# Decay products shifted by one token: transfers of 112 and 15 rows, a second matmul for three chunks, and loads issued at the end of a turn

## The chip, the cores and the metric

The kernel runs on one NeuronCore of a Trainium2 chip. The core has TensorE (PE, with its weight loads PEld), VectorE (DVE), ScalarE (ACT), GpSimd (POOL) and SyncE (SP), and 16 DMA engines that all of them share. The metric is the time of one execution on the device, in microseconds, as the median of several runs. The profile and the trace come from one profiled execution.

## The reference

The first half is a linear attention with a decay (RWKV-6), for 4 batches, 8 heads, 768 tokens and a head size of 48. For every token the state of a head, 48x48, is scaled row by row by `w` and gets `k v` added:

```python
for t in range(S):
    cur = einsum('bhd,bhe->bhde', u[None] * kt, vt)
    y[:, :, t] = einsum('bhd,bhde->bhe', rt, state + cur)
    state = wt[:, :, :, None] * state + einsum('bhd,bhe->bhde', kt, vt)
```

The second half (mixture of depths) takes `y` as `x`, 768 tokens of 384 numbers in each batch. It scores each token by `x @ w_gate`, picks the 128 best of a batch, sends them through `relu(xe @ w1) @ w2` (384 to 1024 to 384), and adds the result, times a sigmoid of the score, to these tokens.

## The kernel before

The 768 tokens of a batch are cut into 6 chunks of 128 tokens (L = 128), so there are N = 24 chunks. A chunk has its tokens on the 128 partitions and 8 heads x 48 in the free dimension: 384 numbers of 4 bytes, 1,536 bytes a row.

The product of decays inside a chunk is made with logarithms. `lnw` takes ln of `w` on ScalarE (L134). `sums` multiplies it on TensorE with the triangular matrix `tri` (L143), which gives for each token the sum of logarithms from that token to the chunk's end. ScalarE takes exp of it as `fall` (L146) and exp of its negative as `rise` (L152). The rows of `fall` then go to two places by DMA:

- L150, issued by ScalarE: rows 1 to 127 of `fall` go to rows 0 to 126 of `e_buf`, since key `t` needs the product of the decays after it. Row 127 of the three `e_buf` tiles is set to 1 once, at the start.
- L151, issued by SyncE: row 0, the decay over the whole chunk, goes to the DRAM tile `lines`. `whole` (L162) reads it back, turned, into `all_buf`, with two transfers for each chunk but a batch's first.

`scaled` (L193) makes K = k x e_buf and R = r x rise on VectorE. `turned` (L204) transposes both on TensorE, ScalarE copies them out (L206). `scores` (L224), `fresh` (L240), `masked` (L252), `states` (L265 to L272, the last one on GpSimd with `all_buf`), `from_state` (L283) and `from_chunk` (L301) make the chunk's output in PSUM. `result` (L323 to L333) writes it out and computes the token scores. `own_products`, `own_sum` and `own_values` do the term with `u`, mostly on GpSimd.

The order is written by hand (`manual_schedule`): every engine runs its instructions in program order. A loop of turns `n` from -4 to 23 does step `turned` for chunk n+2, `scores` to `states` for n+1, `from_state`, `from_chunk` and `result` for n, `scaled` for n+3 and `sums` for n+4, `lnw` for n+5. From turn 6 on, the steps of the second half for the batch before (`mixture`, 28 steps) are spread over the turns, 4 or 5 in each; those of the last batch follow the loop.

SyncE issues in a turn: the four loads of chunk n+8 (L105; `w`, `k`, `r`, `v`, 192 KB each in pieces of 192 bytes), in turns 0 to 6 a slab of the second half's weights (L526), the two `whole` transfers of chunk n+3, the store of chunk n's output (L333), and the row of chunk n+4 (L151). ScalarE issues L150. The head of the program loads chunks 0 to 3 (18 transfers, with `u` and `w_gate`) before the first turn. The tiles for loads have 5 buffers for `w`, 7 for `k` and `r`, 10 for `v`; `fall` and `rise` have 2, `e_buf` 3.

Of the kernel before, what the change touches and what calls it, by code (L numbers as in the profile page):

```python
# [9 lines left out]
FP32 = mybir.dt.float32  # L10
# [3 lines left out]
AF = mybir.ActivationFunctionType  # L14
ALU = mybir.AluOpType
AX = mybir.AxisListType

L = 128
HB = 64
LIMIT = 1e15  # L20


def _rows(ap, n):

    return dataclasses.replace(ap, ap=[[0, n]] + [list(x) for x in ap.ap])
# [10 lines left out]
def kernel(  # L36
# [14 lines left out]
    nc = tc.nc  # L51
# [3 lines left out]
    C = H * D  # L55
# [13 lines left out]
    consts = ctx.enter_context(tc.tile_pool(name="consts", bufs=1))  # L69
# [5 lines left out]
    psR = ctx.enter_context(tc.tile_pool(name="psR", bufs=3, space=PSUM))  # L75
# [3 lines left out]
    N = len(chunks)  # L79
    views = dram_disjoint_views(out, B)  # L80

    lines = dram.tile([N, C], FP32, name="lines")
# [12 lines left out]
    work = {n: {} for n in range(N)}  # L95

    def load(n, names="wkrv"):
        if n >= N:
            return
        b, ci = chunks[n]  # L100
        for name in names:
            x, bufs = dict(w=(w, 5), k=(k, 7), r=(r, 7), v=(v, 10))[name]
            t = lev.tile([L, H, D], FP32, tag=name, name=name, bufs=bufs)
            src = x[b, :, ci * L:(ci + 1) * L, :].rearrange("h t d -> t h d")
            nc.sync.dma_start(out=t, in_=src)  # L105
            work[n][name] = t
# [7 lines left out]

    ident = consts.tile([L, L], FP32)
    tri = consts.tile([L, L], FP32)
    mask = consts.tile([L, HB], FP32)
    ones = consts.tile([L, 1], BF16)
    ones_f = consts.tile([L, 1], FP32)
# [4 lines left out]
    row = setup.tile([L, L], INT32)  # L124
    col = setup.tile([L, L], INT32)
# [4 lines left out]
    def lnw(n):  # L130
        if n < N:
            t = work[n]
            t["lw"] = lev.tile([L, C], FP32, tag="lw", name="lw", bufs=2)
            nc.scalar.activation(  # L134
                out=t["lw"], in_=t.pop("w").rearrange("p h d -> p (h d)"), func=AF.Ln
            )

    def sums(n):
        if not 0 <= n < N:
            return  # L140
        t = work[n]
        ps = psR.tile([L, 512], FP32, tag="r", name="ps_x")
        nc.tensor.matmul(ps[:, 0:C], tri, t.pop("lw"), start=True, stop=True)  # L143
        fall = t["fall"] = lev.tile([L, C], FP32, tag="fall", name="fall")
        rise = t["rise"] = lev.tile([L, C], FP32, tag="rise", name="rise")
        nc.scalar.activation(  # L146
            out=fall, in_=ps[:, 0:C], func=AF.Exp, accum_out=guard[:, n, 0:1]
        )
        e = t["e"] = e_bufs[n % len(e_bufs)]
        nc.scalar.dma_start(out=e[0:L - 1], in_=fall[1:L])  # L150
        nc.sync.dma_start(out=lines[n:n + 1], in_=fall[0:1])  # L151
        nc.scalar.activation(  # L152
            out=rise, in_=ps[:, 0:C], func=AF.Exp, scale=-1.0, accum_out=guard[:, n, 1:2]
        )

    def whole(n):
        if not 0 <= n < N or chunks[n][1] == 0:
            return
        t = work[n]["all"] = all_bufs[n % len(all_bufs)]
        line = lines[n].rearrange("(j q d) -> q d j", q=2, d=D)  # L160
        for par in (0, 1):
            nc.sync.dma_start(out=t[HB * par:HB * par + D, :], in_=line[par])  # L162
# [16 lines left out]
    def own_values(n):  # L179
        if not 0 <= n < N:  # L180
            return
        t = work[n]
        t["vo"] = lev.tile([L, H, D], FP32, tag="vo", name="vo")
        nc.gpsimd.tensor_mul(t["vo"], t["v"], t.pop("own").to_broadcast([L, H, D]))  # L184

    def scaled(n):
        if not 0 <= n < N:
            return
        t = work[n]
        t["K"] = k_bufs[n % len(k_bufs)]  # L190
        t["R"] = r_bufs[n % len(r_bufs)]
        for to, of, by in (("K", "k", "e"), ("R", "r", "rise")):
            nc.vector.tensor_mul(  # L193
                t[to][:, :, 0:D], t.pop(of), t.pop(by).rearrange("p (h d) -> p h d", d=D)
            )
# [18 lines left out]
    def half(i, n=HB):  # L214
        return slice(HB * i, HB * i + n)
# [58 lines left out]
    def from_state(n):  # L274
        if not 0 <= n < N:
            return
        t = work[n]
        begun = set()
        for j in range(HP):
            for par, sub in quarters:  # L280
                if sub == 0 and chunks[n][1] == 0:
                    continue
                nc.tensor.matmul(  # L283
                    t["P"][half(sub), par, j * D:(j + 1) * D],
                    t["Rt"][half(par, D), j, half(sub)],
                    t["s1" if sub else "s0"][half(par, D), j, :],
                    start=(par, sub) not in begun, stop=False, skip_group_check=True,
                )
                begun.add((par, sub))
# [176 lines left out]
    def run(*steps):  # L466
        for g in steps:
            yield from g
# [5 lines left out]
            next(mixing, None)  # L474

    per_turn = [5, 5, 5, 4, 5, 4]
    AHEAD = 8

    with tc.manual_schedule():
        nc.scalar.preload_act_table_set("natural_log_exp_and_others")  # L480
        load(0, "wkr")
        load(1, "wkr")
        nc.sync.dma_start(out=u_bc, in_=_rows(u, L))
        load(0, "v")
        load(1, "v")
        load(2)
        nc.sync.dma_start(out=wg_bc, in_=_rows(moe_w_gate, L))
        load(3)

        nc.gpsimd.iota(row, pattern=[[1, L]], base=0, channel_multiplier=0)  # L490
        nc.gpsimd.iota(col, pattern=[[0, L]], base=0, channel_multiplier=1)
        nc.vector.tensor_tensor(out=tri, in0=col, in1=row, op=ALU.is_ge)
        for t in e_bufs:
            nc.gpsimd.memset(t[L - 32:L], 1.0)
        nc.vector.tensor_tensor(out=ident, in0=col, in1=row, op=ALU.is_equal)
        for t in k_bufs + r_bufs:
            nc.vector.memset(t[:, :, D:HB], 0.0)
        for t in all_bufs:
            nc.gpsimd.memset(t, 1.0)
        nc.vector.tensor_tensor(out=behind[:, 0:L], in0=col, in1=row, op=ALU.is_lt)  # L500
        for i in (0, 1):
            nc.vector.tensor_copy(out=mask[half(i)], in_=behind[half(i), half(i)])
            nc.vector.memset(p_bufs[i], 0.0)
        nc.vector.tensor_copy(out=slots, in_=row)
        nc.vector.memset(ones, 1.0)
        nc.vector.memset(ones_f, 1.0)
        nc.gpsimd.memset(behind[:, L:S], 1.0)
        nc.gpsimd.iota(count, pattern=[[-L, NCH]], base=S - 1, channel_multiplier=-1)
        nc.vector.tensor_copy(out=behind_n, in_=count)
        nc.gpsimd.iota(  # L510
            number[:, :, :, 0], pattern=[[S, B], [L, NCH]], base=0, channel_multiplier=0
        )
        nc.gpsimd.iota(
            number[:, :, :, 1], pattern=[[0, B], [0, NCH]], base=0, channel_multiplier=1
        )
        nc.vector.tensor_copy(out=ids, in_=number)

        lnw(0)
        for n in range(-4, N):
            if n >= 0 and chunks[n][1] == 0 and n > 0:  # L520
                mixing = run(mixing, mixture(chunks[n][0] - 1))
            k1 = per_turn[chunks[n][1]] if n >= NCH else 0
            load(n + AHEAD)
            if n >= 0 and n < len(weights):
                to, of = weights[n]
                nc.sync.dma_start(out=to, in_=of)  # L526
            whole(n + 3)
            lnw(n + 5)
            from_state(n)
            turned(n + 2)  # L530
            scores(n + 1)
            fresh(n + 1)
            own_values(n + 1)
            masked(n + 1)
            states(n + 1)
            mix(k1 // 2)
            from_chunk(n)
            result(n) if n >= 0 else None
            own_products(n + 3)
            own_sum(n + 2)  # L540
            sums(n + 4)
            scaled(n + 3)
            mix(k1 - k1 // 2)
        mixing = run(mixing, mixture(B - 1))
        mix(1000)

        total = setup.tile([L, 1], FP32)
        nc.vector.tensor_reduce(out=total, in_=guard, axis=AX.XY, op=ALU.add)
        ps = psM.tile([L, C], FP32, tag="m", name="ps_w")
        nc.tensor.matmul(ps[0:1, 0:1], total, ones_f, start=True, stop=True)  # L550
        wide = setup.tile([1, 1], INT32)
        nc.vector.tensor_scalar(
            out=wide, in0=ps[0:1, 0:1], scalar1=LIMIT, scalar2=0.5, op0=ALU.is_le, op1=ALU.is_lt
        )
# [72 lines left out]
```

## Time and profile before

| | us |
|---|---|
| median of 3 runs | 379.18 (373.69 to 379.99) |
| the profiled execution | 376.85 |
| its span | 374.8 |
| PE busy | 215.0 (57%) |
| DVE busy | 137.0 (37%) |
| POOL busy | 94.3 (25%) |
| ACT busy | 76.8 (20%) |
| granted TensorE clock, mean | 0.751 of full speed |

The profiled execution took 376.85 us, and 374.8 us of them lie in the span that the trace shows. No engine is busy for much more than half of it. The span falls into a head (until the first chunks are through), 20 turns in which chunks 3 to 23 get their K (from 64.05 us to 317.73 us), and a tail of 57.1 us with the last outputs and the second half of the last batch.

### The profile page before, as it was taken

How to read it: one execution, taken by the hardware profiler on the slowest of the kernel's cores; microseconds unless marked ns; L12 is line 12 of the kernel's file. 1: busy time of each engine (PE TensorE's matmuls, PEld its weight loads, DVE VectorE, ACT ScalarE, POOL GpSimd, SP SyncE). 2: the span in 40 equal slices, each digit the busy share in tenths (PEclk: the TensorE clock that was granted, in tenths of full speed). 3: DMA queues.
4: the chain of work that ended last, by engine and by line, in shares of the span. 5: the costliest groups of instructions: out<-in, count | busy, mean ns of one | idle time of the engine just before them, and what ended most of it. 6: DMA issues, size and time to landing. Idle time of an engine off the chain costs nothing.

```text
span 374.8 us, 8418 instructions
## 1 busy us (share of the span) xinstructions
PE 215.0 (57%) x3586; PEld 168.3 (45%) x3586; DVE 137.0 (37%) x329; ACT 76.8 (20%) x195; POOL 94.3 (25%) x119
## 2 busy tenths in 40 slices
PE   3033252645536745057997337579698647994581
PEld 1023141535425534045865326468465547862460
DVE  4011114404404442615334137353246666326100
ACT  3011411302202321112232221222223211101010
POOL 4300003304307030344330340543215344101101
PEclk9995556875855786565999685669779867997596
DMA  7555716156266515828036542554212111001000
GB/s 149 118 119 118 156 45 130 39 144 163 63 153 160 140 34 112 196 55 194 24 85 137 119 106 63 141 129 91 64 37 64 47 46 51 24 23 42 23 0 30
DMA packets 117100, 34.07 MB, mean 91 GB/s; under 512 B 108864, under 2 KB 116288, under 8 KB 117056
## 3 DMA queue, kind: packets, MB, share of 16 engines
q1 hardware_dynamic: 113472, 27.21, 33.7%
q10 hardware_dynamic: 3072, 4.68, 3.5%
q0 software_dynamic: 512, 1.57, 1.3%
q8 instruction: 30, 0.49, 0.6%
q14 instruction: 14, 0.11, 0.1%
HBM read 23.23 MB, written 5.54 MB: 77 GB/s over the span
## 4 chain that ended last, share of the span: by engine, by line
DMA 47%; PE 24%; issue 5%; SPq 5%; DVE 3%; ACT 2%; POOL 2%; ACTq 0%; POOLq 0%; DVEq 0%
DMA e_buf<-fall 29%; DMA lines<-fall 7%; PE ps_h L440 6%; DMA xe<-out_dram,idx 5%; PE ps_p L301 5%; DMA all_buf<-lines 4%; PE ps_f L450 3%; PE ps_t L204 3%; PE ps_x L143 3%; SPq L162 2%; PE ps_p L224 2%; SPq L105 1%; DVE k_buf L193 1%; PE ps_p L240 1%; DMA w<-in_moe_w_dram 1%
## 5 line engine op out<-in xcount | busy, mean ns | idle before, releaser
L204 PE MATMUL ps_t<-ident,k_buf 128*128 128x128 f32 x96 | 21.6, 366 | 68.4 <-DVE k_buf L193 68.4
L272 POOL TENSOR_TENSOR s<-mid,all_buf 128x192 f32<-128x192 f32 x20 | 10.5, 524 | 186.8 <-DMA all_buf<-lines 127.8
L204 PEld LDWEIGHTS ps_t<-ident,k_buf 128*128 128x128 f32 x96 | 13.9, 182 | 72.9 <-issue 40.5
L252 DVE TENSOR_TENSOR sc<-ps_p,mask 128x512 f32<-128x512 f32 x24 | 16.6, 691 | 65.0 <-PE ps_p L240 64.9
L193 DVE TENSOR_TENSOR k_buf<-k,e_buf 128x384 f32<-128x384 f32 x24 | 14.6, 609 | 64.6 <-DMA e_buf<-fall 64.6
L301 PE MATMUL ps_p<-v,sc 64*64 64x48 f32 x768 | 34.8, 253 | 0.0
L301 PEld LDWEIGHTS ps_p<-v,sc 64*64 64x64 f32 x768 | 32.1, 169 | 5.5 <-issue 4.6
L143 PE MATMUL ps_x<-lw,tri 128*128 128x384 f32 x48 | 28.3, 680 | 8.7 <-ACT lw L134 5.6
L440 PE MATMUL ps_h<-xeT,w 128*128 128x128 f32 x192 | 31.2, 323 | 3.4 <-ACT hid L445 2.8
L283 PE MATMUL ps_p<-s,Rt 48*64 48x48 f32 x704 | 19.3, 247 | 22.5 <-DVE mid L270 15.1
L440 PEld LDWEIGHTS ps_h<-xeT,w 128*128 128x128 f32 x192 | 28.9, 232 | 6.8 <-ACT hid L445 3.6
L146 ACT ACTIVATE fall<-ps_x 128x384 f32<-128x384 f32 x24 | 11.8, 490 | 94.8 <-PE ps_x L143 39.3
L184 POOL TENSOR_TENSOR vo<-v,own 128x384 f32<-128x384 f32 x24 | 22.8, 950 | 33.2 <-DVE own L177 33.1
L283 PEld LDWEIGHTS ps_p<-s,Rt 48*64 48x64 f32 x704 | 16.2, 158 | 32.9 <-POOL s L272 17.6
L450 PE MATMUL ps_f<-w,hid 128*128 128x384 f32 x64 | 25.6, 533 | 2.7 <-ACT hid L445 2.1
L206 ACT COPY Kt<-ps_t 128x512 f32<-128x512 f32 x24 | 14.0, 584 | 64.1 <-PE ps_t L204 64.0
L169 POOL TENSOR_TENSOR rk<-r,k 128x384 f32<-128x384 f32 x24 | 26.0, 1084 | 2.5 <-DMA r<-in_r_dram 2.5
L170 POOL TENSOR_TENSOR rk<-rk,u_bc 128x384 f32<-128x384 f32 x24 | 25.0, 1040 | 5.4 <-DMA u_bc<-in_u_dram 3.6
L323 DVE TENSOR_TENSOR x<-ps_p,vo 128x384 f32<-128x384 f32 x24 | 13.3, 554 | 26.9 <-PE ps_p L301 24.2
L224 PE MATMUL ps_p<-Rt,Kt 48*64 48x64 f32 x768 | 22.8, 279 | 0.0
L224 PEld LDWEIGHTS ps_p<-Rt,Kt 48*64 48x64 f32 x768 | 18.8, 183 | 6.0 <-issue 6.0
L204 PE MATMUL ps_t<-ident,r_buf 128*128 128x128 f32 x96 | 21.1, 361 | 0.2 <-DVE r_buf L193 0.2
(75 smaller groups left out, 271.0 us busy)
## 6 DMA issues: line engine op xcount, KB each, us to landing
w<-in_w_dram SPq DMA_DIRECT2D x24, 192.0 KB
k<-in_k_dram SPq DMA_DIRECT2D x24, 192.0 KB
r<-in_r_dram SPq DMA_DIRECT2D x24, 192.0 KB
v<-in_v_dram SPq DMA_DIRECT2D x24, 192.0 KB
out_dram<-x SPq DMA_DIRECT2D x24, 192.0 KB
e_buf<-fall ACTq DMA_DIRECT2D x24, 190.5 KB
w<-in_moe_w_dram SPq DMA_DIRECT2D x3, 512.0 KB
w<-in_moe_w_dram SPq DMA_DIRECT2D x4, 384.0 KB
```

What stands on the lines that cost most here:

```text
L143: nc.tensor.matmul(ps[:, 0:C], tri, t.pop("lw"), start=True, stop=True)
L169: nc.gpsimd.tensor_mul(rk, t["r"], t["k"])
L170: nc.gpsimd.tensor_mul(rk, rk, u_bc)
L184: nc.gpsimd.tensor_mul(t["vo"], t["v"], t.pop("own").to_broadcast([L, H, D]))
L193: nc.vector.tensor_mul(t[to][:, :, 0:D], t.pop(of), t.pop(by).rearrange("p (h d) -> p h d", d=D))
L204: nc.tensor.transpose(ps[:, j, :], t[name][:, 2 * j:2 * j + 2, :], ident)
L224: nc.tensor.matmul(P[half(sub), par, j * HB:(j + 1) * HB], t["Kt"][half(par, D), j, half(sub)], t["Rt"][half(par, D), j, half(sub)], start ...
L252: nc.vector.tensor_mul(t["sc"], t["P"][:, :, 0:SC].rearrange("p q (j t) -> p q j t", t=HB), _heads(mask, 2, HP),)
L283: nc.tensor.matmul(t["P"][half(sub), par, j * D:(j + 1) * D], t["Rt"][half(par, D), j, half(sub)], t["s1" if sub else "s0"][half(par, D), ...
L301: ins = nc.tensor.matmul(t["P"][half(sub), par, j * D:(j + 1) * D], t["sc"][half(sub), par, j, :], t["v"][half(sub), 2 * j + par, :], star ...
L440: nc.tensor.matmul(ps[:, q, :], w1[:, dc, (f0 + q) * L:(f0 + q + 1) * L], xeT[:, dc, :], start=(dc == 0), stop=(dc == NDC - 1),)
L450: nc.tensor.matmul(ps, hid[:, fc, :], w2[:, fc, :], start=(fc == 0), stop=(fc == NFC - 1))
```

## The change

```diff
--- before.py
+++ after.py
@@ -18,6 +18,7 @@
 L = 128
 HB = 64
 LIMIT = 1e15
+EARLY = 3
 
 
 def _rows(ap, n):
@@ -114,6 +115,7 @@
 
     ident = consts.tile([L, L], FP32)
     tri = consts.tile([L, L], FP32)
+    tri_s = consts.tile([L, L], FP32)
     mask = consts.tile([L, HB], FP32)
     ones = consts.tile([L, 1], BF16)
     ones_f = consts.tile([L, 1], FP32)
@@ -140,18 +142,27 @@
             return
         t = work[n]
         ps = psR.tile([L, 512], FP32, tag="r", name="ps_x")
-        nc.tensor.matmul(ps[:, 0:C], tri, t.pop("lw"), start=True, stop=True)
+        nc.tensor.matmul(ps[:, 0:C], tri, t["lw"], start=True, stop=True)
         fall = t["fall"] = lev.tile([L, C], FP32, tag="fall", name="fall")
         rise = t["rise"] = lev.tile([L, C], FP32, tag="rise", name="rise")
         nc.scalar.activation(
             out=fall, in_=ps[:, 0:C], func=AF.Exp, accum_out=guard[:, n, 0:1]
         )
         e = t["e"] = e_bufs[n % len(e_bufs)]
-        nc.scalar.dma_start(out=e[0:L - 1], in_=fall[1:L])
-        nc.sync.dma_start(out=lines[n:n + 1], in_=fall[0:1])
+        if n < EARLY:
+            strict = psR.tile([L, 512], FP32, tag="r", name="ps_x")
+            nc.tensor.matmul(strict[:, 0:C], tri_s, t["lw"], start=True, stop=True)
+            nc.scalar.activation(out=e, in_=strict[:, 0:C], func=AF.Exp)
+        else:
+            for lo, hi in ((0, L - 16), (L - 16, L - 1)):
+                nc.scalar.dma_start(out=e[lo:hi], in_=fall[lo + 1:hi + 1])
         nc.scalar.activation(
             out=rise, in_=ps[:, 0:C], func=AF.Exp, scale=-1.0, accum_out=guard[:, n, 1:2]
         )
+
+    def line(n):
+        if 0 <= n < N:
+            nc.sync.dma_start(out=lines[n:n + 1], in_=work[n]["fall"][0:1])
 
     def whole(n):
         if not 0 <= n < N or chunks[n][1] == 0:
@@ -474,7 +485,7 @@
             next(mixing, None)
 
     per_turn = [5, 5, 5, 4, 5, 4]
-    AHEAD = 8
+    AHEAD = 7
 
     with tc.manual_schedule():
         nc.scalar.preload_act_table_set("natural_log_exp_and_others")
@@ -492,6 +503,7 @@
         nc.vector.tensor_tensor(out=tri, in0=col, in1=row, op=ALU.is_ge)
         for t in e_bufs:
             nc.gpsimd.memset(t[L - 32:L], 1.0)
+        nc.vector.tensor_tensor(out=tri_s, in0=col, in1=row, op=ALU.is_gt)
         nc.vector.tensor_tensor(out=ident, in0=col, in1=row, op=ALU.is_equal)
         for t in k_bufs + r_bufs:
             nc.vector.memset(t[:, :, D:HB], 0.0)
@@ -520,7 +532,6 @@
             if n >= 0 and chunks[n][1] == 0 and n > 0:
                 mixing = run(mixing, mixture(chunks[n][0] - 1))
             k1 = per_turn[chunks[n][1]] if n >= NCH else 0
-            load(n + AHEAD)
             if n >= 0 and n < len(weights):
                 to, of = weights[n]
                 nc.sync.dma_start(out=to, in_=of)
@@ -539,6 +550,8 @@
             own_products(n + 3)
             own_sum(n + 2)
             sums(n + 4)
+            line(n + 4)
+            load(n + AHEAD)
             scaled(n + 3)
             mix(k1 - k1 // 2)
         mixing = run(mixing, mixture(B - 1))
```

Four things change in it.

1. For chunks 3 to 23 the transfer of 127 rows becomes two, of rows 1 to 112 and 113 to 127, both issued by ScalarE, in place of the one.
2. For chunks 0 to 2 there is no transfer. A second matmul with `tri_s` (strictly greater) gives the sums that leave the token itself out, and ScalarE takes their exp straight into `e_buf`. `tri_s` is one more comparison on VectorE at the start.
3. The row that goes to `lines` is issued by a call of its own, `line(n + 4)`, right behind `sums(n + 4)`: it stays behind the output's store on SyncE's queue.
4. The loads move from the start of a turn to its end, behind `line`, and are of chunk n+7 in place of n+8. In turn -4 that is chunk 3, which the head of the program loads too (L488, not in the diff).

## Rows read from the trace of the kernel before

**Rows 1.** The page: the chain that ended last, shares of the span by line
```profile
DMA e_buf<-fall 29%; DMA lines<-fall 7%; PE ps_h L440 6%; DMA xe<-out_dram,idx 5%; PE ps_p L301 5%; DMA all_buf<-lines 4%; PE ps_f L450 3%; PE ps_t L204 3%; PE ps_x L143 3%; SPq L162 2%; PE ps_p L224 2%; SPq L105 1%; DVE k_buf L193 1%; PE ps_p L240 1%; DMA w<-in_moe_w_dram 1%
```

**Rows 2.** Waits, all engines: engine, line <- releaser: us in total, times, longest
```profile
DVE k_buf L193 <- DMA e_buf<-fall: 64.6, 15, 14.1
```

**Rows 3.** Waits of SyncE's queue, same columns
```profile
SPq L105 <- DMA e_buf<-fall: 45.6, 5, 9.7
```

**Rows 4.** DMA view: queues (packets, MB, share of 16 engines) and issues
```profile
q1 hardware_dynamic: 113472, 27.21, 33.7%
q10 hardware_dynamic: 3072, 4.68, 3.5%
...
e_buf<-fall ACTq DMA_DIRECT2D x24, 190.5 KB
```

**Rows 5.** Chain in order of time: start us, us, what
```profile
178.82 0.61 PE ps_p L283 x32
...
220.85 14.31 DMA e_buf<-fall
...
275.30 10.44 DMA e_buf<-fall
...
337.69 1.85 DMA out_dram<-x
```

**Rows 6.** Windows: per engine busy us (instructions), granted clock, DMA share, GB/s
```profile
0.00:20.00 20.00, 3.29 (x4) 1.00 (x4) 4.49 (x19) 4.37 (x10) 6.84 (x23) 1.00 0.63 127
...
80.00:120.00 40.00, 17.88 (x324) 14.31 (x328) 12.97 (x25) 8.23 (x21) 13.89 (x15) 0.61 0.59 145
...
280.00:300.00 20.00, 15.00 (x326) 11.29 (x317) 12.90 (x27) 5.89 (x16) 7.62 (x9) 0.93 0.17 54
```

**Rows 7.** Timeline, chunk 13's transfer: start, us, engine, line, operation, [idle before]
```profile
186.48 0.61 ACTq L150 DMA_DIRECT2D e_buf<-fall  x1
...
187.10 0.68 PE L283 MATMUL ps_p<-s,Rt 48*64 48x48 f32 x32
...
195.76 2.68 SPq L333 DMA_DIRECT2D out_dram<-x  x1
...
198.44 0.56 DVE L193 TENSOR_TENSOR k_buf<-k,e_buf 128x384 f32<-128x384 f32 x1 [3.18 <-DMA e_buf<-fall]
...
204.59 0.49 ACT L146 ACTIVATE fall<-ps_x 128x384 f32<-128x384 f32 x1 [2.52 <-PE ps_x L143]
```

**Rows 8.** Timeline: k_buf products of chunks 3, 4, 5, 6 and 19 to 23
```profile
64.05 0.70 DVE L193 TENSOR_TENSOR k_buf<-k,e_buf 128x384 f32<-128x384 f32 x1
...
73.35 0.56 DVE L193 TENSOR_TENSOR k_buf<-k,e_buf 128x384 f32<-128x384 f32 x1 [1.86 <-DMA e_buf<-fall]
...
88.43 0.70 DVE L193 TENSOR_TENSOR k_buf<-k,e_buf 128x384 f32<-128x384 f32 x1
...
98.84 0.56 DVE L193 TENSOR_TENSOR k_buf<-k,e_buf 128x384 f32<-128x384 f32 x1 [1.98 <-DMA e_buf<-fall]
...
274.67 0.55 DVE L193 TENSOR_TENSOR k_buf<-k,e_buf 128x384 f32<-128x384 f32 x1
...
285.76 0.56 DVE L193 TENSOR_TENSOR k_buf<-k,e_buf 128x384 f32<-128x384 f32 x1 [0.44 <-DMA e_buf<-fall]
...
295.71 0.56 DVE L193 TENSOR_TENSOR k_buf<-k,e_buf 128x384 f32<-128x384 f32 x1 [2.14 <-DMA e_buf<-fall]
...
304.33 0.56 DVE L193 TENSOR_TENSOR k_buf<-k,e_buf 128x384 f32<-128x384 f32 x1 [0.85 <-DMA e_buf<-fall]
...
317.73 0.55 DVE L193 TENSOR_TENSOR k_buf<-k,e_buf 128x384 f32<-128x384 f32 x1
```

**Rows 9.** Groups by form: prefix-sum matmuls, busy us, mean ns, idle before
```profile
L143 PE MATMUL ps_x<-lw,tri 128*128 128x384 f32 x48 | 28.3, 680 | 8.7 <-ACT lw L134 5.6 <-ACT rise L152 3.1
```

**Rows 10.** Timeline, head: chunk 2's w load and its ln
```profile
7.71 2.89 SPq L105 DMA_DIRECT2D w<-in_w_dram  x1
...
18.90 0.52 ACT L134 ACTIVATE lw<-w 128x384 f32<-128x384 f32 x1 [9.31 <-DMA w<-in_w_dram]
```

## Prediction, made before the changed kernel was run

> **What bounds the kernel now.** I read the chain of work that ended last first. No engine leads it: the transfer `e_buf<-fall` holds 29% of the span, some 109 us, and the one-row transfer to `lines` 7% [rows 1]. The reader is to see that this is a latency, since the waits say the same from the other side: VectorE stood 64.6 us before its k_buf product, 15 times, for this transfer alone [rows 2]. SyncE's queue, which loads the next chunks, is also put down as waiting for it, 45.6 us [rows 3].
>
> Why is it slow? The queue table answers [rows 4]. ScalarE's queue, q10, did 3,072 packets for 24 transfers: 128 each, that is 127 rows and one more. On q1, I counted the pieces of data: 98,304 for 96 loads, 3,072 for stores, 7,680 for `all_buf` (40 transfers of 192 numbers), 384 + 1,024 for the weights, 256 for the two broadcasts and 24 for `lines`, in all 110,744. What is left of 113,472 is 2,728, and that is exactly 16 for each of 169 transfers and 1 for each of 24 one-row transfers. So a transfer leaves one closing packet on each DMA engine that it uses. A load uses 16, a single row one, and the 127 rows one as well. A q10 packet took 3.5% x 16 x 374.8 / 3,072 = 68 ns, so 128 of them take 8.75 us on one engine. With some 1.7 us around them that is the 10.44 us of the quietest case; beside loads it is up to 14.31 [rows 5].
>
> That one DMA engine is full. In the first 20 us loads moved 127 x 20 = 2,540 KB, less 195 of chunk 0's shifted rows: 147 KB on each engine, 763 pieces of 192 B. A q1 packet took 33.7% x 16 x 374.8 / 113,472 = 17.8 ns, so that is 13.6 us; with 8.75 it is 22 us of work in 20 for the one engine, and about 14 for the others, whose mean share was 0.63 [rows 6]. So loads end late there too.
>
> The timeline of chunk 13 shows the way it goes around: issued at 186.48, landed at 198.44 (12.0), k_buf, and 6.2 us later the next-but-one `fall` at 204.59, which needs that turn's transposes and matmuls before it on TensorE. The store at 195.76 is held 2.68 us, to the moment when chunk 13's rows land, though it doesn't read them [rows 7]. In program order it is the eighth transfer of SyncE and ScalarE behind them. I read this as eight completion counters used in turn.
>
> **The change, part by part.**
>
> *Two transfers for one.* 112 rows divide evenly over 16 engines, as the loads' 128 do, 15 don't. The nearest row for a transfer that uses 16 is the store of 128 rows of the same 1,536 bytes: 1.85 us [rows 5]; that is the lower bound. The upper one is no change, 12. The 15 rows, on one engine, cost 15 x 68 ns = 1.0 on top of 1.7, and their issue waits 0.61 for the first one's [rows 7]. Sum: 0.6 + 2.7, about 3.5 us with some contention. I take that, because beside loads the old transfer gained at most 14.31 - 10.44 = 3.9 us over 128 packets, 30 ns each, and the new one has 8 on an engine. ScalarE gains one issue, 0.61 us in a turn, under its 20% busy time.
>
> The Trainium skill, "DMA: Bandwidth & Descriptors", section "Why a DMA increments its semaphore by 16 and not by 1", says that a transfer uses the largest number of engines up to 16 that divides its slowest dimension, so 16 for 112 and 15 for 15; its 127 to 1 agrees with the closing packets [rows 4]. By it the second part costs 0.9 us less, and the sum would be the same, since neither price sets the turn. Speaking against the change, "Queues, rings and completion order" there says that an engine goes around its queues by packets of about 9 to 17 descriptors; seven packets would then wait 1.1 to 2.1 us (9 to 17 times 17.8 ns, an estimate), which is small too.
>
> The loop around it falls from 12.0 + 6.7 (with the exp's 0.5) to 3.5 + 6.7 = 10.2 us for two turns, 5.1 a turn. Turns took (317.73 - 64.05) / 20 = 12.7 [rows 8], so something else is late next: TensorE's own turn.
>
> *A turn without that wait.* I take the waits out of measured turns. Without the second half: chunks 3 to 4, 9.30 - 1.86 = 7.4, and 5 to 6, 10.41 - 1.98 = 8.4 [rows 8]; mean 7.9. Weight slabs load there (7 slabs, 3.1 MB, at full rate up to 2.2 us a turn); I add 0.9 of these 0 to 2.2. Six turns: 6 x 8.8 = 53 (48 to 61). With the second half, a batch of six: 9.95 - 2.14 = 7.8, 8.62 - 0.85 = 7.8 and 13.4 (the gather stall, which stays) [rows 8], twice 8.28 (from state product to state product, 178.82 to 187.10) [rows 5, 7], and 11.09 - 0.44 = 10.7 [rows 8]: 56.2. I take 57 (54 to 60) with loads beside it, two times. The last two turns, 22.0 - 0.85 = 21. The tail stays at 374.8 - 317.73 = 57.
>
> *Head.* Three transfers of 127 rows go, so the full DMA engine goes. Added are three pairs of matmuls, 0.68 each [rows 9], three exps at 0.49 and one comparison: some 2 us for each chunk, under the wait for `w` (9.31 before chunk 2's ln [rows 10]); uncovered it is 6 us. Chunk 3 is loaded twice, 786 KB. Before turn 0's copies ScalarE takes ln of chunk 5, behind 18 + 4 + 4 + 1 = 27 transfers of 196.6 KB, 5.31 MB. The rate at full share is 127 / 0.63 = 202 GB/s [rows 6]: 26 us at share 1, 42 at 0.63. I take 0.85, 31 us, and 5 for the start and turn 0: chunk 3's k_buf at 36 (29 to 44), against 64.05.
>
> *Loads two chunks later.* SyncE's order stays (row, loads, weights, `whole`, store), only the chunk is two lower, and `w` comes one turn and a bit before its ln. The worst `w` took from 7.71 to 18.90 = 11.2 us [rows 10], with the full engine; a turn covers 8 of it, and without cover it would cost 3 a turn. Nothing in the sum. With ten transfers in a turn the eighth-before rule makes the 15 rows wait for `w` of the turn before, with `rise`, ln and the copies queued behind it on ScalarE; it was issued a turn earlier, so nothing either.
>
> Sum: 36 + 53 + 57 + 57 + 21 + 57 = 281 us of span, against 374.8. With 2.05 around it (376.85 - 374.8) the profiled time would be 283; the median stands 2.3 above the profiled one, so 286.
>
> **Rivals.**
>
> *The DMA engines become the bound.* Both queues did 37.2% x 374.8 = 139 us of work for 16 engines; the second load of chunk 3 adds 4. At the head's share of 0.63 to 0.65 [rows 6] this takes 220 us up to chunk 23's loads, which chunk 21's turn needs at 203 in my sum: 225 + 21 + 57 + 4 = 308; at 0.59 [rows 6] 330. For it: loads come in a burst behind each turn's end. Against: the share was low because one engine was full.
>
> *It doesn't spread.* If the parts still run on one engine or a few, only the head's 28 us are gained: 351. Against: the loads' closing packets.
>
> *Quicker.* TensorE had a granted clock of 0.61 from 80 to 120 us, with waits in it, and 0.93 from 280 to 300 [rows 6]. With the clock at 2.4 GHz nearly throughout, turns fall to 7: 29 + 42 + 50 + 50 + 20 + 55 + 4 = 250.
>
> *Slower: `w` comes too late.* From the loads' issue to ln is one turn, and behind ln ScalarE has the copies, `fall` and so the next row and loads: two turns take the latency of `w` plus 7. To be slower than now by 2% (387) turns must take (387 - 4 - 36 - 57) / 20 = 14.5, a latency of 22 us. At 24 it would be 407. The longest measured is 11.2 [rows 10].
>
> **How the numbers follow.** Chances: forecast (272 to 302) 0.62; DMA bound (300 to 330) 0.19; quicker (250 to 272) 0.09; no spread (340 to 360) 0.07; slower 0.03. The predicted time is 286; the range 264 to 322 takes in most of the second and half of the third. About 2% is what a measurement here can tell from no change. All but the last are faster by more: 0.94; within 2% 0.03, for a `w` late by nearly that much; slower 0.03.
>
> **What would show it.** ScalarE's queue should show closing packets of 16 for the 112 rows, and the time from its issue to k_buf some 3.5 us; the e_buf wait should leave the top of the chain, with PE lines in its place. Chunk 3's k_buf should stand near 36 us, turns near 8.8 and 9.5. Wrong would be: waits of k_buf on `e_buf` as long as before, ln waiting for `w` in every turn, or a DMA share near 0.65 throughout with TensorE waiting.

## The result and the profile after

The changed kernel takes 280.81 us, the median of 4 runs (279.03 to 286.5); the kernel before took 376.55 in the runs beside it. The ratio is 0.746, with a 95% interval of 0.734 to 0.758. The forecast was 286 (264 to 322). The profiled execution has a span of 277.2 us, where the sum gave 281.

The page of the changed kernel, first the engines' busy time and then the chain that ended last, by line (L204 is now the k_buf product, L215 the transposes, L106 the loads, L136 ln):

```profile
PE 201.8 (73%) x3592; PEld 153.6 (55%) x3592; DVE 141.2 (51%) x330; ACT 76.9 (28%) x198; POOL 96.8 (35%) x119
...
PE ps_t L215 6%; SPq L106 6%; PE ps_h L451 6%; DMA w<-in_w_dram 5%; PE ps_p L312 5%; PE ps_p L235 4%; PE ps_f L461 4%; DVE r_buf L204 4%; DVE ahead L369 3%; PE ps_x L145 3%; DVE k_buf L204 3%; PE ps_p L251 3%; DVE x L334 2%; DMA e_buf<-fall 2%; DVE sc L263 2%
```

The transfer of shifted rows, 29% of the chain before [rows 1], stands at 2%. In its place several lines of TensorE, VectorE and SyncE's queue stand close together, none above 6%. The DMA view of the same kernel (queue: packets, MB, share of 16 engines' span):

```profile
q1 hardware_dynamic: 117632, 28.00, 47.0%
q10 hardware_dynamic: 3318, 4.10, 5.1%
```

3,318 packets on ScalarE's queue are 158 for each of 21 chunks: 127 rows and 31 closing packets. With at most 16 a transfer, that is 16 for the 112 rows and 15 for the 15 rows. A packet takes 5.1% x 16 x 277.2 / 3,318 = 68 ns, as before [rows 4], so nothing got faster; the rows run side by side. On q1 there are 4,160 packets more than before: 4 x (1,024 + 16), the second load of chunk 3.

Two transfers from the chain in order of time (start us, us, what), and a load for comparison:

```profile
45.36 2.37 DMA e_buf<-fall
...
61.38 3.84 DMA e_buf<-fall
...
68.31 6.25 DMA w<-in_w_dram
```

The two pairs that stand in the chain are through after 2.4 and 3.8 us, against 10.4 to 14.3 for the one transfer [rows 5]. The waits (engine, line <- releaser: us in total, times, longest):

```profile
ACT lw L136 <- DMA w<-in_w_dram: 23.0, 8, 7.2
POOL s L283 <- DMA all_buf<-lines: 22.8, 4, 9.1
...
PE ps_t L215 <- DVE k_buf L204: 9.3, 12, 1.5
```

The wait of the k_buf product for the transfer, 64.6 us before [rows 2], is gone from the list; TensorE waits 9.3 us for k_buf in all. What is at the top of the waits for transfers now is `w`: ln stood 23.0 us for it. GpSimd's wait for `all_buf`, the way of the one-row transfer, was the longest of all before and has shrunk as well, from 127.8 us to 22.8. The line of the kernel before:

```profile
POOL s L272 <- DMA all_buf<-lines: 127.8, 9, 37.9
```

The timeline gives the time of the k_buf product of chunks 3, 9, 15, 21 and 23:

```profile
36.34 0.88 DVE L204 TENSOR_TENSOR k_buf<-k,e_buf 128x384 f32<-128x384 f32 x1
...
86.89 0.55 DVE L204 TENSOR_TENSOR k_buf<-k,e_buf 128x384 f32<-128x384 f32 x1
...
141.92 0.54 DVE L204 TENSOR_TENSOR k_buf<-k,e_buf 128x384 f32<-128x384 f32 x1
...
196.61 0.54 DVE L204 TENSOR_TENSOR k_buf<-k,e_buf 128x384 f32<-128x384 f32 x1
...
217.96 0.54 DVE L204 TENSOR_TENSOR k_buf<-k,e_buf 128x384 f32<-128x384 f32 x1
```

And the windows (busy us and instructions of PE, PEld, DVE, ACT and POOL, then granted clock, DMA share, GB/s):

```profile
0.00:36.00 36.00, 18.64 (x248) 11.74 (x248) 13.73 (x38) 12.93 (x34) 12.41 (x30) 0.81 0.90 176
36.00:87.00 51.00, 42.46 (x802) 32.38 (x802) 26.53 (x55) 16.61 (x44) 19.64 (x22) 0.67 0.78 184
87.00:142.00 55.00, 44.84 (x896) 34.77 (x896) 34.78 (x78) 18.76 (x48) 27.02 (x28) 0.91 0.76 171
```

The DMA engines' share reached 0.90 in the head, where it was 0.63 in the first 20 us before [rows 6]. In the head TensorE is busy for 18.6 of 36 us, and the loads keep the DMA engines nearly full.

### The profile page after: what moved, and what is told of

Read it like the earlier page. It is cut to its first block, busy times and chain, and to the rows that moved or that the text cites. A ratio compares the mean times of both kernels' runs of the same rounds, so it can differ in the third digit from the quotient of the medians.

```text
span 277.2 us, 8475 instructions
## 1 busy us (share of the span) xinstructions
PE 201.8 (73%) x3592; PEld 153.6 (55%) x3592; DVE 141.2 (51%) x330; ACT 76.9 (28%) x198; POOL 96.8 (35%) x119
## 3 DMA queue, kind: packets, MB, share of 16 engines
q10 hardware_dynamic: 3318, 4.10, 5.1%
## 4 chain that ended last, share of the span: by engine, by line
PE 35%; DVE 21%; issue 15%; DMA 12%; SPq 9%; ACT 4%; POOL 1%; ACTq 1%; DVEq 0%; POOLq 0%
PE ps_t L215 6%; SPq L106 6%; PE ps_h L451 6%; DMA w<-in_w_dram 5%; PE ps_p L312 5%; PE ps_p L235 4%; PE ps_f L461 4%; DVE r_buf L204 4%; DVE ahead L369 3%; PE ps_x L145 3%; DVE k_buf L204 3%; PE ps_p L251 3%; DVE x L334 2%; DMA e_buf<-fall 2%; DVE sc L263 2%
## 5 line engine op out<-in xcount | busy, mean ns | idle before, releaser
L312 PE MATMUL ps_p<-v,sc 64*64 64x48 f32 x768 | 32.2, 242 | 6.2 <-ACT Kt L217 6.2
L312 PEld LDWEIGHTS ps_p<-v,sc 64*64 64x64 f32 x768 | 29.3, 157 | 11.4 <-ACT Kt L217 6.8
L451 PE MATMUL ps_h<-xeT,w 128*128 128x128 f32 x192 | 27.8, 299 | 3.4 <-ACT hid L456 2.8
L451 PEld LDWEIGHTS ps_h<-xeT,w 128*128 128x128 f32 x192 | 25.3, 208 | 6.0 <-ACT hid L456 3.6
L215 PE MATMUL ps_t<-ident,r_buf 128*128 128x128 f32 x96 | 19.7, 341 | 8.4 <-ACT e_buf L155 5.0
L461 PE MATMUL ps_f<-w,hid 128*128 128x384 f32 x64 | 23.7, 501 | 2.7 <-ACT hid L456 2.1
L215 PE MATMUL ps_t<-ident,k_buf 128*128 128x128 f32 x96 | 18.6, 326 | 9.3 <-DVE k_buf L204 9.3
L204 DVE TENSOR_TENSOR r_buf<-r,rise 128x384 f32<-128x384 f32 x24 | 21.7, 905 | 0.0
L159 ACT ACTIVATE rise<-ps_x 128x384 f32<-128x384 f32 x24 | 11.8, 491 | 33.0 <-DVE k_buf L204 15.6
L235 PE MATMUL ps_p<-Rt,Kt 48*64 48x64 f32 x768 | 20.8, 262 | 0.0
L215 PEld LDWEIGHTS ps_t<-ident,r_buf 128*128 128x128 f32 x96 | 13.5, 172 | 11.6 <-ACT e_buf L155 5.4
```

The source lines that it names most:

```text
L204: nc.vector.tensor_mul(t[to][:, :, 0:D], t.pop(of), t.pop(by).rearrange("p (h d) -> p h d", d=D))
L215: nc.tensor.transpose(ps[:, j, :], t[name][:, 2 * j:2 * j + 2, :], ident)
L235: nc.tensor.matmul(P[half(sub), par, j * HB:(j + 1) * HB], t["Kt"][half(par, D), j, half(sub)], t["Rt"][half(par, D), j, half(sub)], start ...
L312: ins = nc.tensor.matmul(t["P"][half(sub), par, j * D:(j + 1) * D], t["sc"][half(sub), par, j, :], t["v"][half(sub), 2 * j + par, :], star ...
L451: nc.tensor.matmul(ps[:, q, :], w1[:, dc, (f0 + q) * L:(f0 + q + 1) * L], xeT[:, dc, :], start=(dc == 0), stop=(dc == NDC - 1),)
L461: nc.tensor.matmul(ps, hid[:, fc, :], w2[:, fc, :], start=(fc == 0), stop=(fc == NFC - 1))
```

## Experiments

The theory: the transfer of 127 rows sat on one DMA engine, and its 8.75 us there cost twice. Its rows came late, and its engine held up the share of every load that must pass it. Rivals: the second matmul or the new place of the loads gave the gain; the lateness alone did; and for what bounds the kernel now, TensorE or the DMA engines.

### Which part of the change gave the gain

`split_only` is the kernel before with the first part of the change alone, for all chunks:

```diff
-        nc.scalar.dma_start(out=e[0:L - 1], in_=fall[1:L])
+        for lo, hi in ((0, L - 16), (L - 16, L - 1)):
+            nc.scalar.dma_start(out=e[lo:hi], in_=fall[lo + 1:hi + 1])
```

> The kernel before with one edit: every chunk's 127 rows go in transfers of 112 and 15; loads, row and early chunks as before. If the one DMA engine that carried 127 rows is the cause, nearly all of the gain is here: 282 to 295 us. If the second matmul of the early chunks or the later loads gave it, 340 us and more.

285.45 us, ratio 0.752 (0.745 to 0.760). Its queue of ScalarE in the DMA view:

```profile
q10 hardware_dynamic: 3792, 4.68, 5.5%
```

These are 24 x 158 packets. Within the intervals this is the whole gain; the other three parts together bring too little to be told apart from nothing. The head is there too: chunk 3's k_buf stands at 40.39 us, where it stood at 64.05 [rows 8] and stands at 36.34 with all four parts.

```profile
40.39 0.71 DVE L194 TENSOR_TENSOR k_buf<-k,e_buf 128x384 f32<-128x384 f32 x1
```

`one_of_127` is the reverse, the changed kernel with the one transfer back:

```diff
-            for lo, hi in ((0, L - 16), (L - 16, L - 1)):
+            for lo, hi in ((0, L - 1),):
```

> The changed kernel with the rows of chunks 3 to 23 in one transfer of 127 again; all else stays. If that transfer is the cause, only the head's gain is left, 340 to 360 us. If the place and distance of the loads gave the gain, under 300 us.

362.71 us, ratio 0.958 (0.950 to 0.966). The queue, the waits and the window from 36 to 87 us:

```profile
q10 hardware_dynamic: 2688, 4.10, 3.1%
```

```profile
ACT lw L136 <- DMA w<-in_w_dram: 72.9, 12, 14.5
...
DVE k_buf L204 <- DMA e_buf<-fall: 38.7, 13, 5.0
```

```profile
36.00:87.00 51.00, 25.84 (x479) 20.89 (x479) 12.86 (x31) 9.98 (x26) 13.58 (x17) 0.58 0.49 117
```

2,688 is 21 x 128: one closing packet, one engine. Between 36 and 87 us the DMA share is 0.49, where the changed kernel has 0.78. And ln waits 72.9 us for `w`, three times as long as with the pair, though `w` stands at the same place in the program. Two things can make these loads late, and this run doesn't part them: one of their 16 engines is full, and SyncE's queue, which issues them, stood 56.0 us (6 waits) for `e_buf` transfers, against 19.6 us (10 waits) in the changed kernel. The largest entry of these is the one in front of the loads:

```profile
SPq L106 <- DMA e_buf<-fall: 29.0, 3, 10.3
```

The rival "it doesn't spread" had 351 us for this case (340 to 360). It is 12 us more. Chunk 3's k_buf is at 41.06 us, some 5 us later than with the pair, and the 20 turns to chunk 23 take 260.3 us, where they took 253.7 before: with loads issued two chunks later, one transfer of 127 rows costs more than that sum allowed for.

`early_0` takes the second matmul out (`EARLY = 0`), so chunks 0 to 2 use the pair of transfers too.

> The changed kernel with transfers of 112 and 15 rows for chunks 0 to 2 too, in place of the second matmul. If the head gained because the full DMA engine is gone, 281 to 287 us: the transfer's 3 us stand under the wait for the next w. If the matmuls themselves gave the head's 28 us, 295 us and more.

285.11 us, ratio 0.749 (0.740 to 0.758): not to be told from the changed kernel. Chunk 3's k_buf is 1.1 us later than with the matmuls:

```profile
37.48 1.34 DVE L204 TENSOR_TENSOR k_buf<-k,e_buf 128x384 f32<-128x384 f32 x1
```

So the head's gain of 28 us came with the spread transfers, not with the matmuls.

### Lateness or a filled engine

`two_engines` cuts the rows at 118 (`L - 10` in place of `L - 16`).

> The changed kernel with the rows cut as 118 and 9. 118 is divided by 2 and by no other number up to 16, so two engines should carry 59 rows each, 4.0 us, and the landing should take about 6 us in place of 3.5. A product a turn later has some 8 us for it. If the old transfer cost by its latency alone, 279 to 285 us; if the filling of the engine that carries it counts too (4.0 us of rows beside 5 to 6 us of loads and stores in turns of 8.4), 287 to 296 us.

301.01 us, ratio 0.797 (0.790 to 0.805). The queue, and the wait of ln for `w`:

```profile
q10 hardware_dynamic: 2898, 4.10, 4.9%
```

```profile
ACT lw L136 <- DMA w<-in_w_dram: 46.8, 8, 10.3
```

2,898 is 21 x 138: 127 rows, 2 closing packets for 118 rows and 9 for 9. So the time grows with the rows on the fullest engine, at most 8, at most 60 and 127: 281, 301 and 363 us. But lateness and filling grow together here.

`spare_61` is to part them. It adds a transfer that nobody waits for; `spare_64` is the same with 64 rows:

```diff
+    spares = [consts.tile([L, C], FP32, name=f"spare{i}") for i in range(4)]
...
+            nc.scalar.dma_start(out=spares[n % 4][0:61], in_=wg_bc[0:61])
```

> The changed kernel with one more transfer behind the two, for chunks 3 to 23: 61 rows, which only one engine can carry (4.1 us), from a constant into tiles that nobody reads. No work waits for its data. If filling one engine costs, since every load waits for that engine's share, 286 to 296 us; if only the latency of the shifted rows counted, 279 to 285 us.

> The same spare transfer with 64 rows, which go to 16 engines, 4 each. The issue and the place among the transfers are as with 61. 279 to 285 us by either theory of the data; as slow as with 61 rows, if the issue on ScalarE or one more transfer in the count is what costs.

306.99 us (0.814, 0.807 to 0.821) with 61 rows, and 285.62 us (0.759, 0.751 to 0.766) with 64. The queue and the window from 36 to 87 us, first with 61 rows:

```profile
q10 hardware_dynamic: 4620, 6.07, 6.5%
```

```profile
36.00:87.00 51.00, 29.48 (x636) 23.19 (x628) 17.25 (x40) 11.54 (x33) 16.00 (x19) 0.67 0.67 157
```

Then with 64:

```profile
q10 hardware_dynamic: 4998, 6.16, 7.5%
```

```profile
36.00:87.00 51.00, 37.02 (x734) 28.96 (x734) 24.44 (x49) 15.54 (x41) 19.95 (x22) 0.70 0.77 185
```

4,620 is 21 x (158 + 61 + 1), 4,998 is 21 x (158 + 64 + 16). The second kernel moves more bytes and is 21.4 us quicker. In the first, the DMA engines move 157 GB/s instead of 185. A transfer on one engine costs, though nobody uses its data. Where the time goes shows in the waits, first with 61 rows:

```profile
POOL s L285 <- DMA all_buf<-lines: 63.5, 9, 11.1
...
ACT lw L137 <- DMA w<-in_w_dram: 34.6, 10, 7.7
```

Then with 64:

```profile
ACT lw L137 <- DMA w<-in_w_dram: 25.0, 9, 6.7
...
POOL s L285 <- DMA all_buf<-lines: 12.3, 3, 6.5
```

So it isn't only the loads over 16 engines that come late. GpSimd waits five times as long for `all_buf`, which comes by way of the one-row transfer to `lines`, and that transfer uses one engine too.

One limit of this pair: if eight counters are used in turn, as the prediction read it, a spare that lands late can also hold the transfer eight places behind it. The traces narrow this down. SyncE's queue stood no longer for the transfers of ScalarE, rows and spares together (18.6 us with 61 rows, 20.8 with 64). But ScalarE, behind its three issues, waited 57.5 us in 21 waits before `rise`, against 47.6. By these lists some 10 of the 21.4 us can be held issues; for the rest the filled engine is the explanation left.

`two_hops` was to make the rows late without filling an engine: they go into a spare tile first and then, both times as 112 and 15, into `e_buf`, issued by ScalarE behind the second exp.

```diff
...
+        if n >= EARLY:
+            for lo, hi in ((0, L - 16), (L - 16, L - 1)):
+                nc.scalar.dma_start(out=e[lo:hi], in_=hops[n % 3][lo:hi])
```

> The changed kernel with the shifted rows of chunks 3 to 23 sent twice in a row, first into a spare tile and from there, behind the exp of the negative sums, into e_buf, each time as 112 and 15 rows. The rows come some 4 us later (about 7.5 us in all, more than the 6 us of the cut at 118), and every engine gets only 0.5 us more to do. If the lateness of the rows is what cost with the cut at 118, 295 us and more; if it was the filled engines, 281 to 290 us (two more issues on ScalarE and two more transfers in the count included).

315.2 us (311.02 to 319.05), against 376.53 of the kernel before beside it. Two waits of it:

```profile
PE ps_p L316 <- ACT Kt L221: 20.3, 9, 4.5
...
ACT lw L137 <- DMA hop<-fall: 18.0, 6, 3.8
```

This doesn't answer the question. In no wait of its list did k_buf stand for the rows. ScalarE, which runs in order, stood in front of its second issue until the first hop had landed, and so ln and the copies behind it came late, and TensorE's `from_chunk` after them. The edit brought a wait of its own.

`late_rows` has SyncE issue the second hop, behind the loads of the turn's end (`second(n + 4)` after `load(n + AHEAD)`), so ScalarE doesn't wait.

> The changed kernel with the shifted rows of chunks 3 to 23 sent into a spare tile by ScalarE, and from there into e_buf by SyncE, behind the loads of that turn's end, both times as 112 and 15 rows. The second hop waits for the first (3.5 us) and then stands behind some 4 us of loads on the same queue, so the rows land some 9 to 11 us after their exp, nearly as late as the 12 us of one transfer of 127, but no engine gets more than about 0.6 us more to do, and ScalarE waits for nothing more. If filling one engine was the whole cost, 281 to 292 us; if the rows' lateness alone sets the turns, 310 to 345 us; between them, both.

293.86 us (292.43 to 294.73), against 379.26 beside it. Chunk 3 in its timeline: first hop, second hop, k_buf:

```profile
28.92 2.00 ACTq L159 DMA_DIRECT2D hop<-fall  x2
...
35.73 2.97 SPq L167 DMA_DIRECT2D e_buf<-hop  x2
...
41.20 0.56 DVE L210 TENSOR_TENSOR k_buf<-k,e_buf 128x384 f32<-128x384 f32 x1 [5.39 <-DMA e_buf<-hop]
```

12.3 us lie between issue and use, as much as with one transfer of 127 rows before [rows 7], and k_buf waits 5.39. Yet the kernel is only 13 us slower than the changed one. The rows were this late in the first turns only, up to chunk 8, where loads stand ahead of them on the queue; from some 90 us on k_buf no longer waited for them. For chunks 3 to 8 k_buf waited for its rows each time, so these turns can be compared with those of the one late transfer. Chunk 9's k_buf, first with the late rows, then with the one transfer of 127 (`one_of_127`):

```profile
98.87 0.55 DVE L210 TENSOR_TENSOR k_buf<-k,e_buf 128x384 f32<-128x384 f32 x1
```

```profile
120.45 0.56 DVE L204 TENSOR_TENSOR k_buf<-k,e_buf 128x384 f32<-128x384 f32 x1 [3.05 <-DMA e_buf<-fall]
```

In the changed kernel it stands at 86.89. So up to there the late rows cost 12 us and the transfer on one engine 34: most of it isn't lateness of the rows. How the remaining part of the 82 us in all divides in the later turns, where `late_rows` had no late rows, stays open.

### What bounds the kernel now

`early_24` makes the second matmul for all chunks (`EARLY = 24`); no shifted row goes by DMA.

> The changed kernel with the second matmul for all 24 chunks and no transfer of shifted rows at all. TensorE gets 0.9 to 1.65 us more in each of 21 turns (0.91 at the higher clock). If TensorE now sets the turns, 296 to 306 us; if the DMA engines or the rows' way still set them, 275 to 283 us.

273.63 us (273.27 to 279.1), ratio 0.726 (0.720 to 0.733): quicker than the changed kernel, with 21 pairs of matmuls more. The window from 36 to 87 us:

```profile
36.00:87.00 51.00, 41.79 (x954) 30.98 (x947) 35.67 (x70) 22.73 (x59) 26.51 (x28) 0.90 0.91 207
```

The DMA share is 0.91 at 207 GB/s (0.78 and 184 with the transfers) and the granted clock 0.90 (0.67). The k_buf products of chunks 9 and 23, and the window from chunk 3's to chunk 9's, the six turns that take from 36 to 87 us in the changed kernel:

```profile
80.44 0.55 DVE L204 TENSOR_TENSOR k_buf<-k,e_buf 128x384 f32<-128x384 f32 x1
...
214.73 0.54 DVE L204 TENSOR_TENSOR k_buf<-k,e_buf 128x384 f32<-128x384 f32 x1
```

```profile
36.11:80.44 44.33, 35.12 (x793) 26.29 (x786) 29.03 (x54) 18.97 (x48) 24.32 (x25) 0.90 0.92 212
```

Chunk 9's k_buf comes 6.4 us earlier than in the changed kernel. In these six turns TensorE is busy for 35.1 us in place of 42.5, with the added matmuls and at the higher clock. From there to chunk 23, where the clock was high in both, the kernel takes 3.2 us more (134.3 against 131.1). Whether the clock stood higher because the matmuls fill gaps or because the waits for rows are gone, these runs don't part. What is shown is that the volume of loads was not the limit of the first turns: they went faster, at 207 GB/s, when the rows were out of their way.

`ahead_8` loads chunk n+8 at a turn's end (`AHEAD = 8`), so chunk 3 comes once. `ahead_9` loads n+9 there, and chunk 4 in the head. `load_3_once` keeps n+7 and leaves the second load of chunk 3 out.

> The changed kernel with chunk n+8 in place of n+7 at the end of a turn, so chunk 3 is loaded once. ScalarE waited 23.0 us in 8 waits for w in the changed kernel. If these set the early turns, 270 to 277 us; if other work there would have been late anyway, 279 to 282 us.

> The changed kernel with chunk n+9 at the end of a turn and chunk 4 added to the head's loads, which is the lookahead of the kernel before. With n+8 the waits for w had left the list's top, so a further chunk should give little: 274 to 279 us. If a w was still late in the first turns, 268 to 273 us; if the longer head delays the first rows to DRAM, 280 to 286 us.

> The changed kernel without the second load of chunk 3 at the end of turn -4; chunk n+7 otherwise as it is. The 786 KB take some 4 us of all 16 engines in a stretch where their share was 0.88 to 0.95. If that load is what the lookahead of n+8 saved, 276 to 279 us; if it was the distance, 280 to 283 us.

277.24 us (0.728, 0.719 to 0.736), 281.34 us (0.747, 0.741 to 0.753), and 282.5 us with runs from 270.19 to 286.34. One chunk more of distance may bring 3 to 7 us (by the medians and by the ratios), though its interval overlaps the changed kernel's; two bring nothing that can be told. What the second load of chunk 3 costs can't be told from runs that lie this far apart. `early_24` is the version whose interval lies below that of the changed kernel.

## Why the prediction was right

| part of the sum | forecast, us | measured, us |
|---|---|---|
| head, to k_buf of chunk 3 | 36 | 36.3 |
| six turns without the second half (to chunk 9) | 53 | 50.6 |
| a batch of six (to chunk 15) | 57 | 55.0 |
| a batch of six (to chunk 21) | 57 | 54.7 |
| last two turns (to chunk 23) | 21 | 21.4 |
| tail | 57 | 59.2 |
| span | 281 | 277.2 |

**The cause.** The closing packets named it before any run: 128 packets for 127 rows, one engine. `split_only` and `one_of_127` show that this transfer, taken alone, makes the difference. By which way it costs is shown in part: late rows are the smaller share of it (`late_rows`), and a full engine and held issues are not wholly parted. The Trainium skill, "DMA: Bandwidth & Descriptors", section "Why a DMA increments its semaphore by 16 and not by 1", says that the largest number up to 16 that divides the row count is used. Every count here agrees: 16 and 15 closing packets for 112 and 15 rows, 2 and 9 for 118 and 9, 1 for 127 and for 61, 16 for 64.

**The 15 rows.** The sum put them on one engine, 2.7 us. They used 15. It changed nothing: the two pairs in the chain took 2.4 and 3.8 us, where 3.5 was forecast.

**The full engine.** That one engine was full and held the loads was worked out from the head's share, 0.63; afterwards the share was 0.90, close to the 0.85 that the head's term took. This step carried the head, and the spare transfers bear it out, with the limit named there. One price in it is too high: 17.8 ns is the mean of all packets of q1, the stores' and weights' larger ones too. At 17.8 ns, 16 full engines would move 173 GB/s in pieces of 192 bytes, where the prediction itself has 202. With one engine full, the share of 0.63 leaves the others 12.1 us for their 763 pieces, 15.9 ns each; the one engine then has 20.9 us of work in 20, still full.

**The turns.** Taking the wait out of measured turns gave each stretch within 3 us. For the first six turns this is partly luck: the sum took two turns, 9.30 and 10.41 us, and left out the 15.08 between them (73.35 to 88.43 [rows 8]) without a reason. With it the mean is 10.3 in place of 7.9, and six turns with the 0.9 come to 67, above the term's own 61. Nor was the reason given for these terms right everywhere. The prediction let TensorE's own turn follow as the limit. Between 87 and 142 us that fits: it was busy for 44.8 of 55 us with a granted clock of 0.91. Between 36 and 87 us it was as busy, but the clock was 0.67 and ln waited 5.1 us for `w`; more work on it and no transfer made these turns shorter (`early_24`).

**The loads.** The 11.2 us of the worst `w` [rows 10] were put down as nothing, since a turn covers most. Measured were 23.0 us of waits for `w`, 8 times, so the term was not nothing; it lay inside the turn times that were forecast. `ahead_8` puts its worth at 3 to 7 us, if it is worth anything.

**The rivals.** "DMA engines become the bound" took the old share of 0.63 to 0.65 as the best there is. With the pair the share is 0.90 in the head and 0.78 behind it, and with the one transfer back it falls to 0.49 there (`one_of_127`), so the low share came with that transfer. "It doesn't spread" fell with the closing packets. "Slower" would have needed a `w` 22 us late; the longest load in the chain took 6.25 us, and ln's longest wait for `w` was 7.2. "Quicker" had the clock right for the later turns, 0.91 between 87 and 142 us, but not what it brings: the two batches of six took 55.0 and 54.7 us, not 50. The chances of the four faster cases add up to 0.97, not to the 0.94 that was given.

## What to carry to other kernels

Look at how many engines a transfer uses before looking at its size: here 127 and 61 rows ran on one and 118 on two, and the count of packets beyond the rows shows it. Such a transfer cost even where nobody waited for it (21.4 us with the 61 spare rows a turn), since loads and one-row transfers beside it came late; cut it into a part that divides by 16 and a rest. Where a small matmul can make the shifted data, it may be quicker still than any transfer.

## What was not expected of the hardware

A kernel with 21 pairs of matmuls more on TensorE, and no transfers of rows, was 7 us quicker, with the granted clock at 0.90 in place of 0.67 between 36 and 87 us. A transfer of 61 rows that nobody reads cost 21.4 us more in all than one of 64 rows. And an issue that waits on ScalarE's queue cost more (`two_hops`, some 30 us) than rows that came 12 us after their issue in the first turns (`late_rows`, 13 us).
